# Where a split w_out lives, and from which block on the down products are made of parts

## The chip, the cores and the metric

The kernel runs on one core of a Trainium2 chip. The core has five engines that run side by side, each with its own queue of instructions in a fixed order: TensorE (PE in the profile, with its weight loads as PEld), VectorE (DVE), ScalarE (ACT), GpSimd (POOL) and SyncE (SP, which only starts transfers here). They wait for one another by semaphores. SBUF is the on-chip memory that all of them work on. PSUM is a small memory of eight banks into which TensorE writes its sums. The metric is the time of one execution on the device, in microseconds (us).

## The reference

Two stages follow one another. The first is an attention with polynomial sketches over q, k and v of shape (4 batches, 4 heads, 1088 positions, 32). The second is a feed-forward block with 128 inputs, 1536 hidden units and 128 outputs on all 4 x 1088 = 4352 tokens.

```
a, b  = S1 x, S2 x                      # 8 numbers each, for q and for k
phi   = outer(a, b)                     # 64 features
kv    = phi(k)^T v ;  z = sum phi(k)    # per batch and head
x     = (phi(q) kv) / (phi(q) z + 1e-6) # then (batch, head, pos, d) -> (token, 128)
out   = (silu(x w_gate) * (x w_val)) w_out
```

All inputs are float32 in the reference, with weights that may arrive as 64-bit floats. The result is float32.

## The kernel before, in words

The 4352 tokens are cut into blocks. Batch 0 makes three blocks of 384, 320 and 384 tokens. The other 3264 tokens make six blocks of 480 and one of 384. These seven are the list `line`, and `line[0]` is the first block of 480. The hidden units are cut into 12 chunks of 128, numbered j. For a pair (block i, chunk j) the gate and value products give 128 hidden units for the tokens of the block, and the down product adds their share to the outputs.

TensorE takes a float32 product in several passes (in the trace, two matmul instructions, `L1077`). It takes the type float32r in one pass, but with fewer bits. So the kernel writes some products as three products of parts. With CUT = 1 - 2^-13, BETA = 4096 and WHOLE = 1 + 1/4096, a number x becomes x1 = round(CUT x), x0 = x - x1 and xd = WHOLE x1 - x. A weight w becomes w1 = round(CUT w), wb = BETA (w - w1) and wd = w1 - wb. Then w x is WHOLE (w1 x1 + wb x0) - wd xd. The gate and value products of all blocks of `line` are made this way: `start_unit` (L983) makes the product of differences (L989), which ACT scales in PSUM (L992), and `finish_unit` (L994) adds the other two (L1001, L1002). ACT then makes the silu (L1004), and DVE the product of both sides, which is the hidden chunk (L1009).

The list `DOWN` (L888) says which down products are made of parts too. Before the change these are six chunks of `line[2]`, nine of each of `line[3]` to `line[5]`, and seven of the last block, 40 in all. For these, `cut_hidden` (L951) cuts the hidden chunk: ACT or DVE makes h1 (L968, L966), POOL h0 (L969) and DVE hd (L972). In `down` (L1054) three one-pass matmuls follow (L1069, L1071, L1072), into two PSUM banks. One of these holds the parts `wd hd`, along with the plain down products of the same block. As the parts enter the result with a minus sign, the plain ones have to be made of negated weights; these are kept in `scaled`. The other bank holds the rest, is copied out by ACT with the factor WHOLE (`copy_out`, L1095), and DVE joins both (`put_together`, L1105). A block without parts has one bank and goes straight to `store`, where DVE transposes it (L1131) and SP sends it off. All other down products are plain float32 (L1077).

`cut_down` (L903) cuts ten of the twelve chunks of w_out (`FINE`), in steps y = 20 to 29.

The order of all work is written out by hand. The loop at the end (`for y in range(END)`) has a step y for each pair of `line` and j, 84 in all: y = 0 to 11 belong to `line[0]`, 12 to 23 to `line[1]`, and so on. A step y puts on the queues: the start of unit y+1, the finish of unit y, and one down product. The down product lags five steps behind its hidden chunk (`len(todo) > min(5 + ...)`, with one step more before the first of `line[1]`, so that at y = 18 two are made). `add_to(before, y + 1, f)` and `add_to(behind, y + 1, f)` put work ahead of or behind the ACT and DVE work of a later step. A hidden chunk of step y that is cut gets h1 in step y + 1, h0 in y + 2 and hd in y + 3.

Between these, the attention of batches 1 to 3 is woven in by the generator `attentions` (L615): `parts_of` takes one piece of it in each step up to y = 19, then in every second step. At y = 4, 6, 20, 22 and 40 (`GROUPS`) come its matmuls. DVE makes the features (L377, in `key_features`), POOL adds them up (`feature_sums`, L547), and `query_step` makes the query side (L741 to L758). The token parts x1, x0, xd of the next block are cut in `cut_tokens` (L865, L868, L873).

The units' PSUM: `pair` (L122) hands out the least lately used of three pairs of banks. The pair of a unit comes free when DVE has made the product (L1009), and the unit three steps on writes the same pair. Bank `acc` and bank `g2` hold the down sums. Both `line[0]` and `line[1]` put theirs into `acc`; a block with parts uses both banks, and consecutive later blocks swap the two.

SBUF is full, so buffers are used again under a name (`tag`): a tile with the tag of an older one waits until that one has been read. Before the change, the parts of w_out live in the tag `room` (an early scratch), their low part in `late` (ten late hidden slots), `scaled` in `zs`. The parts of hidden chunks live in six sets of three slots in the tags `kld`, `qld`, `vld`, `kT`, `qT` (keys, queries, values and their transposes) and `late`.

Of the kernel before, what the change touches and what calls it, by code (L numbers as in the profile page):

```python
# [19 lines left out]
def kernel(  # L20
# [28 lines left out]
    nc = tc.nc  # L49
# [100 lines left out]
    wg = const.tile([P, NCH, P], FP32, name="wg")  # L150
    wv = const.tile([P, NCH, P], FP32, name="wv")
# [162 lines left out]
    slots = [(hbuf[:, k, :] if k < NH - NL else late[:, k - NH + NL, :]) for k in range(NH)]  # L314
# [300 lines left out]
    def attentions():  # L615
# [54 lines left out]
        for b in (2, 3):  # L670
# [232 lines left out]
    def cut_down():  # L903

        n = len(FINE)
        parts = const.tile([P, 3, n, D], F32R, tag="room", name="dparts", bufs=1)
        w1, wb, wd = (parts[:, k] for k in range(3))
        scaled = apool.tile([P, len(PLAIN), D], FP32, tag="zs", name="scaled")
        low = const.tile([P, n, D], FP32, tag="late", name="dlow", bufs=1)
        down_parts.update(w1=w1, wb=wb, wd=wd, scaled=scaled)  # L910
        rest = [(0, slice(0, 1)), (1, slice(1, 8, 2)), (5, slice(6, 7)), (6, slice(NCH - 1, NCH))]

        def high(c):
            nc.scalar.activation(w1[:, c], wo[:, FINE[0] :][:, c], AF.Copy, scale=CUT)

        def left(c):
            nc.gpsimd.tensor_tensor(
                out=low[:, c], in0=wo[:, FINE[0] :][:, c], in1=whole(w1[:, c]), op=ALU.subtract
            )

        def scale(c):
            nc.scalar.activation(wb[:, c], low[:, c], AF.Copy, scale=BETA)

        def differ(c):
            nc.gpsimd.tensor_tensor(
                out=wd[:, c], in0=whole(w1[:, c]), in1=whole(wb[:, c]), op=ALU.subtract
            )

        def other(k, c):
            m = len(range(NCH)[c])  # L930
            nc.scalar.activation(scaled[:, k : k + m, :], wo[:, c, :], AF.Copy, scale=-1.0)


        def exchange():
            for k, c in zip((1, 3, 4), (8, 9, 10)):
                PLAIN[k] = c
                nc.scalar.activation(scaled[:, k, :], wo[:, c, :], AF.Copy, scale=-1.0)

        add_to(behind, NCH * 5 + 8, exchange)

        a, b, c = slice(0, 3), slice(3, 6), slice(6, n)
        for step in (
            [(high, a)], [(left, a), (high, b)], [(left, b), (scale, a)], [(differ, a), (high, c)],
            [(left, c), (scale, b)], [(differ, b), (scale, c)], [(differ, c), (other, *rest[0])],
            [(other, *rest[1])], [(other, *rest[2]), (other, *rest[3])],
        ):
            for f, *args in step:
                f(*args)
            yield

    def cut_hidden(y, i, j):  # L951

        if not h_sets:
            x = []
# [450 lines left out]
    for y in range(END):  # L1405
# [16 lines left out]
        if y in range(20, 30):  # L1422
            next(down_steps, None)
# [43 lines left out]
```

## Time and profile before

| | before |
|---|---|
| time, median of 3 runs | 276.71 us (276.70 to 277.21) |
| span of the profiled execution (the page gives no other time for it) | 275.1 us |
| PE busy | 268.8 us, 98% |
| PEld busy | 200.5 us, 73% |
| DVE busy | 214.1 us, 78% |
| ACT busy | 193.6 us, 70% |
| POOL busy | 105.7 us, 38% |
| TensorE clock granted | 0.999 |
| plain down products on `hbuf` (L1077), 128x480 | 565 ns for each of two instructions, overlapping |
| products of parts (L1069, L1071, L1072), 128x480 | 379 to 382 ns each, overlapping |

Matmuls are pipelined: the duration of one is longer than the distance to the next. What a piece of work on the PE costs is therefore read from the starts in the chain of waits, and not from the mean durations. The chain of waits is followed back from the last instruction, and a line of it is a start, a length, an engine and a line of the kernel. A timeline lists an engine's instructions in order of time; the brackets at the end say how long the engine was idle before the instruction, and what ended that idle time.

### The profile page before, as it was taken

What the parts mean: (1) busy time and instruction counts of PE and PEld (TensorE: products, weight loads), DVE (VectorE), ACT (ScalarE), POOL (GpSimd) and SP (SyncE); (2) the same over time, 40 slices, a digit from 0 to 9 for tenths busy, and PEclk for the clock granted to TensorE, in tenths of its full rate; (3) what the DMA queues carried; (4) which work ended last, traced back from release to release, by engine and by line L of the source; (5) the groups of instructions that cost most, each with busy time, mean ns of one, the idle gap of its engine ahead of it and who ended that gap; (6) DMA issues with size and microseconds to landing.
All of it is one profiled execution on the core that took longest, in us unless ns stands there. A gap on an engine that the chain in (4) does not pass through costs nothing.

```text
span 275.1 us, 5788 instructions
## 1 busy us (share of the span) xinstructions
PE 268.8 (98%) x2191; PEld 200.5 (73%) x2191; DVE 214.1 (78%) x373; ACT 193.6 (70%) x349; POOL 105.7 (38%) x117
## 2 busy tenths in 40 slices
PE   7999999999999999999999999999999999999995
PEld 6645566666785786777577777867887888789994
DVE  3997988989788773887545766967987995998871
ACT  2468666462685686677479898769879888897880
POOL 3313422149350640260034353435535663553330
PEclk9999999999999999999999999999999999999999
DMA  6573196122231043000200020000100200010021
GB/s 191 172 216 87 49 270 200 60 104 62 62 88 23 4 111 99 2 0 0 38 12 4 1 38 0 0 2 11 26 2 0 36 1 0 13 25 1 2 36 29
DMA packets 26139, 14.30 MB, mean 52 GB/s; under 512 B 19840, under 2 KB 24192, under 8 KB 26112
## 3 DMA queue, kind: packets, MB, share of 16 engines
q1 hardware_dynamic: 25456, 13.84, 19.6%
q8 instruction: 17, 0.28, 0.4%
q10 hardware_dynamic: 656, 0.10, 0.2%
q14 instruction: 10, 0.08, 0.1%
HBM read 11.41 MB, written 2.23 MB: 50 GB/s over the span
## 4 chain that ended last, share of the span: by engine, by line
PE 93%; DVE 3%; DMA 2%; ACT 1%; issue 0%; SPq 0%
PE PS L1077 20%; PE PS L1001 14%; PE PS L989 14%; PE PS L1002 14%; PE PS L1025 12%; PE PS L1072 3%; PE PS L1071 3%; PE PS L1069 3%; PE PS L354 2%; PE PS L776 2%; PE PS L342 2%; DMA kld<-in_k_dram 2%; PE PS L388 2%; PE PS L1117 1%; PE PS L497 1%; PE PS L445 1%
## 5 line engine op out<-in xcount | busy, mean ns | idle before, releaser
L992 ACT ACTIVATE PS<-PS 128x960 f32<-128x960 f32 (+1 forms) x90 | 83.3, 926 | 29.8 <-PE PS L989 28.8
L1009 DVE SCALAR_TENSOR_TENSOR hbuf<-PS,sg 128x480 f32<-128x480 f32 (+1 forms) x87 | 55.2, 634 | 36.6 <-ACT sg L1004 36.1
L1004 ACT ACTIVATE sg<-PS 128x480 f32<-128x480 f32 (+1 forms) x90 | 49.6, 551 | 1.6 <-PE PS L1002 1.2
L1077 PE MATMUL PS<-hbuf,wo 128*128 128x480 f32 (+2 forms) x94 | 39.4, 516 | 0.0
L989 PE MATMUL PS<-xd,graw 128*128 128x480 f32 (+1 forms) x69 | 37.5, 543 | 0.0
L989 PE MATMUL PS<-xd,wd 128*128 128x480 f32 (+1 forms) x90 | 33.6, 373 | 0.0
L1002 PE MATMUL PS<-x,wb 128*128 128x480 f32 (+1 forms) x90 | 33.5, 372 | 0.0
L1001 PE MATMUL PS<-x,w 128*128 128x480 f32 (+1 forms) x90 | 33.4, 371 | 0.0
L1002 PE MATMUL PS<-x,graw 128*128 128x480 f32 (+1 forms) x69 | 25.5, 370 | 0.0
L989 PEld LDWEIGHTS PS<-xd,wd 128*128 128x128 f32 x90 | 17.0, 189 | 9.9 <-issue 5.3
L1025 PE MATMUL PS<-xT,wg 128*128 128x384 f32 (+1 forms) x60 | 23.5, 473 | 0.1
L1025 PE MATMUL PS<-xT,wv 128*128 128x384 f32 (+1 forms) x60 | 23.2, 467 | 0.3 <-DVE wv L286 0.3
L868 POOL TENSOR_TENSOR x<-xT,x 128x480 fp32r<-128x480 f32 (+1 forms) x6 | 7.2, 1195 | 37.8 <-ACT x L865 37.8
L1077 PEld LDWEIGHTS PS<-hbuf,wo 128*128 128x128 f32 x94 | 17.7, 189 | 5.4 <-issue 0.4
L1029 ACT ACTIVATE sg<-PS 128x384 f32<-128x384 f32 (+1 forms) x24 | 11.2, 468 | 13.2 <-PE PS L1025 12.4
L969 POOL TENSOR_TENSOR hlate<-hbuf,hlate 128x480 fp32r<-128x480 f32 (+1 forms) x12 | 14.6, 1218 | 11.0 <-ACT hlate L968 9.7
L989 PEld LDWEIGHTS PS<-xd,graw 128*128 128x128 f32 x69 | 13.0, 188 | 7.6 <-ACT PS L992 4.1
L1001 PEld LDWEIGHTS PS<-x,w 128*128 128x128 f32 x90 | 16.9, 187 | 2.2
L1002 PEld LDWEIGHTS PS<-x,wb 128*128 128x128 f32 x90 | 16.9, 188 | 2.1
L1001 PE MATMUL PS<-x,graw 128*128 128x480 f32 (+1 forms) x48 | 18.1, 376 | 0.0
L1077 PE MATMUL PS<-hbuf,scaled 128*128 128x480 f32 (+1 forms) x40 | 17.1, 518 | 0.0
L1025 PEld LDWEIGHTS PS<-xT,wv 128*128 128x128 f32 x60 | 11.2, 190 | 7.4 <-DVE hbuf L1040 0.8
(205 smaller groups left out, 572.0 us busy)
## 6 DMA issues: line engine op xcount, KB each, us to landing
kld<-in_k_dram SPq DMA_DIRECT2D x4, 544.0 KB, 4.4
vld<-in_v_dram SPq DMA_DIRECT2D x12, 144.0 KB, 4.3
qld<-in_q_dram SPq DMA_DIRECT2D x3, 544.0 KB, 4.8
raw<-in_moe_w_out_dram SPq DMA_DIRECT2D x4, 384.0 KB, 4.4
raw<-in_moe_w_gate_dram SPq DMA_DIRECT2D x3, 384.0 KB, 3.3
raw<-in_moe_w_val_dram SPq DMA_DIRECT2D x3, 384.0 KB, 3.5
out_dram<-o SPq DMA_DIRECT2D x16, 60.0 KB, 2.0
vld<-in_v_dram SPq DMA_DIRECT2D x4, 112.0 KB, 4.1
```

What stands on the lines that cost most here:

```text
L969: add_to(before, y + 2, lambda: nc.gpsimd.tensor_tensor(out=h0, in0=h, in1=whole(h1), op=ALU.subtract))
L989: nc.tensor.matmul(ps[:, k], w_parts[id(w), j // 3][2][:, j % 3, :], xd, start=True, stop=True)
L992: nc.scalar.activation(ps, ps, AF.Copy, scale=-1.0 / WHOLE)
L1001: nc.tensor.matmul(ps[:, k], w1, x1, start=False, stop=False, skip_group_check=True)
L1002: nc.tensor.matmul(ps[:, k], wb, x0, start=False, stop=True, skip_group_check=True)
L1004: nc.scalar.activation(sg, ps[:, 0], AF.Silu, scale=WHOLE)
L1009: nc.vector.scalar_tensor_tensor(out=hj[:, 0:n], in0=ps[:, 1], scalar=WHOLE, in1=sg, op0=ALU.mult, op1=ALU.mult)
L1025: nc.tensor.matmul(o[:, 0:n], w[:, j, :], xT[:, t0 : t0 + n], start=True, stop=True)
L1029: nc.scalar.activation(sg[:, 0:n], g[:, 0:n], AF.Silu)
L1069: nc.tensor.matmul(acc[i][:, 0:n], wd, hd, **sides)
L1071: nc.tensor.matmul(p, w1, h1, start=(j == mine[0]), stop=False)
L1077: nc.tensor.matmul(acc[i][:, 0:n], w, hidden[i, j][:, 0:n], **sides)
```

## The change

Three things are done together. The parts of w_out move into `wg` and `wv`, the buffers of the gate and value weights, which have been read out by then (their own parts lie elsewhere), and `zs`; their low part gets a buffer of its own, `low`, taken from `room`. They are cut in five pieces from y = 5, 6, 13, 14 and 23 on. The difference of weights is made with the other sign, wb - w1, so that plain products need no negated weights: `scaled` and its copies go, and the join becomes a plain addition. The parts of hidden chunks get seven sets (five before `line[2]`) in `room`, `late`, `kld` + `kT`, `kT` + `qld`, `vld` + `qT` and `feats`; `feats` is the part of `late` that had held the features of batch 3. With this, `DOWN` gets three chunks of `line[0]`, five of `line[1]`, and nine of `line[2]` where there were six: 51 in all. Both `line[0]` and `line[1]` now use the two banks and a join. In `line[0]` and `line[2]` DVE makes h1 of chunk 8, in `line[1]` of 6, 8 and 10; ACT makes the others.

Lines after the change are 15 or 16 lower from `cut_hidden` on: L974 and L977 for L989 and L992, L989 for the silu L1004, L994 for the unit product L1009, L950, L948, L951 and L954 for the cuts of hidden chunks, L1054, L1056, L1057 and L1061 for the down products, L1079, L1089 and L1113 for copy, join and transpose. L910, L912, L914 and L916 are the cuts of w_out.

```diff
-    wg = const.tile([P, NCH, P], FP32, name="wg")
-    wv = const.tile([P, NCH, P], FP32, name="wv")
+    wg = const.tile([P, NCH, P], FP32, tag="wg", name="wg", bufs=1)
+    wv = const.tile([P, NCH, P], FP32, tag="wv", name="wv", bufs=1)
...
-    NL = 10
+    NL, NF = 10, 6
-    late = const.tile([P, NL, BW], FP32, tag="late", name="late", bufs=1)
+    late = const.tile([P, NL - NF, BW], FP32, tag="late", name="late", bufs=1)
+    feats = const.tile([P, NF, BW], FP32, tag="feats", name="feats", bufs=1)
...
-                phk = late[:, NL - 6 :, :].rearrange("p s (n h i j) -> p (s n) h i j", h=1, i=R, j=R)
+                phk = feats[:].rearrange("p s (n h i j) -> p (s n) h i j", h=1, i=R, j=R)
...
-    FINE, PLAIN = range(1, NCH - 1), [0, 1, 3, 5, 7, 6, NCH - 1]
-    DOWN = [(line[2], j) for j in (2, 4, 6, 8, 9, 10)]
-    DOWN += [(i, j) for i in line[3:6] for j in (1, 2, 4, 5, 6, 7, 8, 9, 10)]
+    DOWN = [(line[0], j) for j in (6, 8, 10)] + [(line[1], j) for j in range(6, 11)]
+    DOWN += [(i, j) for i in line[2:6] for j in (1, 2, 4, 5, 6, 7, 8, 9, 10)]
...
+    def cut_down(c0, c1, home, low):
+        n = c1 - c0
+        w1, wb, wd = (home[:, n * k : n * k + n, :] for k in range(3))
+        for k in range(n):
+            down_parts[c0 + k] = [x[:, k, :] for x in (w1, wb, wd)]
+        src = wo[:, c0:c1, :]
+        nc.scalar.activation(w1, src, AF.Copy, scale=CUT)
+        yield
+        nc.gpsimd.tensor_tensor(out=low, in0=src, in1=whole(w1), op=ALU.subtract)
+        yield
+        nc.scalar.activation(wb, low, AF.Copy, scale=BETA)
+        yield
+        nc.gpsimd.tensor_tensor(out=wd, in0=whole(wb), in1=whole(w1), op=ALU.subtract)
+
+    def more_room():
+        def ground(tag, n):
+            t = const.tile([P, n, WB], F32R, tag=tag, name="h" + tag, bufs=1)
+            return [t[:, k, :] for k in range(n)]
+        x = ground("room", 6)
+        yield x[:3]
+        yield x[3:]
+        yield ground("late", 3)
+        x = ground("kld", 2) + ground("kT", 2)
+        yield x[:3]
+        x = x[3:] + ground("qld", 2)
+        yield x
+        x = ground("vld", 2) + ground("qT", 2)
+        yield x[:3]
+        yield ground("feats", 4)[:3]
...
-        if not h_sets:
...
+        if len(h_sets) < (5 if i < line[2] else OWN):
+            h_sets.insert(0, next(h_rooms))
...
-        if j in (2, 5, 8, 10) and i != line[2]:
+        if j in ((2, 5, 8, 10) if i > line[2] else (6, 8, 10) if i == line[1] else (8,)):
...
-            w1, wb, wd = [down_parts[x][:, FINE.index(j), :] for x in ("w1", "wb", "wd")]
+            w1, wb, wd = down_parts[j]
...
-            w = down_parts["scaled"][:, PLAIN.index(j), :] if mine else wo[:, j, :]
-            nc.tensor.matmul(acc[i][:, 0:n], w, hidden[i, j][:, 0:n], **sides)
+            nc.tensor.matmul(acc[i][:, 0:n], wo[:, j, :], hidden[i, j][:, 0:n], **sides)
...
-        join = lambda: nc.vector.scalar_tensor_tensor(
-            out=x, in0=d, scalar=-1.0, in1=x, op0=ALU.mult, op1=ALU.add
-        )
+        join = lambda: nc.vector.tensor_tensor(out=x, in0=d, in1=x, op=ALU.add)
...
-    down_steps = cut_down()
+    for y0, c0, c1, where in (
+        (5, 5, 8, ("wg", 0)), (6, 8, 11, ("wv", 0)), (13, 4, 5, ("wg", 9)), (14, 1, 2, ("wv", 9)),
+        (23, 2, 4, ("zs", 0)),
+    ):
+        for k in range(4):
+            down_steps.setdefault(y0 + k, []).append((k, c0, c1, *where))
...
-        if y in range(20, 30):
-            next(down_steps, None)
+        for k, c0, c1, tag, t0 in down_steps.get(y, ()):
+            if k == 0:
+                n = c1 - c0
+                parts_at = settle(tag, NCH if tag != "zs" else 6)[:, t0 : t0 + 3 * n, :]
+                low_at = settle("low", 6)[:, 3 * (c0 >= 8) :, :][:, 0:n, :]
+                cutting[c0] = cut_down(c0, c1, parts_at, low_at)
+            next(cutting[c0], None)
```

More of the change, by code (lines that the diff above doesn't have):

```diff
@@ L310 @@
     NH = 27
-    NL = 10
+    NL, NF = 10, 6
     hbuf = const.tile([P, NH - NL, BW], FP32, name="hbuf")
-    late = const.tile([P, NL, BW], FP32, tag="late", name="late", bufs=1)
-    slots = [(hbuf[:, k, :] if k < NH - NL else late[:, k - NH + NL, :]) for k in range(NH)]
+    late = const.tile([P, NL - NF, BW], FP32, tag="late", name="late", bufs=1)
+    feats = const.tile([P, NF, BW], FP32, tag="feats", name="feats", bufs=1)
+    slots = [x[:, k, :] for x, n in ((hbuf, NH - NL), (late, NL - NF), (feats, NF)) for k in range(n)]
     slot_of = {}
@@ L901, in now @@
             f()
[L903 to L918, printed above, removed]
-            )
[L921 to L949, printed above, removed]
@@ L951, in cut_hidden @@
-    def cut_hidden(y, i, j):
-        if not h_sets:
-            x = []
-            for tag in ("kld", "qld", "vld", "kT", "qT"):
-                t = const.tile([P, 2, WB], F32R, tag=tag, name="h" + tag, bufs=1)
-                x += [t[:, k, :] for k in range(2)]
-            t = const.tile([P, 8, WB], F32R, tag="late", name="hlate", bufs=1)
-            x += [t[:, k, :] for k in range(8)]
-            h_sets.extend(x[k : k + 3] for k in range(0, 18, 3))
+    def cut_down(c0, c1, home, low):
[11 more added lines that the diff above has]
+        nc.gpsimd.tensor_tensor(out=wd, in0=whole(wb), in1=whole(w1), op=ALU.subtract)
@@ L961, in cut_hidden @@
+    h_rooms = more_room()
+    OWN = 7
+    def cut_hidden(y, i, j):
+        if len(h_sets) < (5 if i < line[2] else OWN):
+            h_sets.insert(0, next(h_rooms))
         n = SPLIT if i == LAST else blocks[i][1]
@@ L974, in cut_hidden @@
         ))
-    room = const.tile([P, 10, BW], FP32, tag="room", name="room", bufs=1)
+    rooms = [
+        const.tile([P, n, BW], FP32, tag=tag, name=tag, bufs=1) for tag, n in (("room", 8), ("low", 2))
+    ]
+    room = [x[:, k, :] for x, n in zip(rooms, (8, 2)) for k in range(n)]
     sums_of = {}
@@ L1027, in unit @@
             )
-        sg = room[:, len(lates) + caught[0], :] if late else fpool.tile([P, WB], FP32, tag="sg", name="sg", bufs=5)
+        sg = room[len(lates) + caught[0]] if late else fpool.tile([P, WB], FP32, tag="sg", name="sg", bufs=5)
         nc.scalar.activation(sg[:, 0:n], g[:, 0:n], AF.Silu)
@@ L1104, in put_together @@
         acc[i] = x
-        join = lambda: nc.vector.scalar_tensor_tensor(
-            out=x, in0=d, scalar=-1.0, in1=x, op0=ALU.mult, op1=ALU.add
-        )
+        join = lambda: nc.vector.tensor_tensor(out=x, in0=d, in1=x, op=ALU.add)
         if i == LAST:
@@ L1294, in free @@
     def free(c):
-        return [room[:, c, :].rearrange("p (c f) -> p c f", f=P)]
+        return [room[c].rearrange("p (c f) -> p c f", f=P)]
     w = ("wg", "wv")
@@ L1403, with settle @@
             token_steps.setdefault(at, []).append(gen)
-    down_steps = cut_down()
+    home = {}
+    def settle(tag, n=NCH):
+        if tag not in home:
+            pool = apool if tag == "zs" else const
+            home[tag] = pool.tile([P, n, D], FP32 if tag == "low" else F32R, tag=tag, name="d" + tag, bufs=1)
+        return home[tag]
+    down_steps = {}
+    for y0, c0, c1, where in (
[4 more added lines that the diff above has]
+            down_steps.setdefault(y0 + k, []).append((k, c0, c1, *where))
+    cutting = {}
     for y in range(END):
```

## The prediction

> **What bounds the kernel now.** I read the page first, for busy shares and clock, then the chain of waits in order of time, then the timelines of PE, DVE and POOL around the blocks that change.
>
> ```profile
> PE 268.8 (98%) x2191; PEld 200.5 (73%) x2191; DVE 214.1 (78%) x373; ACT 193.6 (70%) x349; POOL 105.7 (38%) x117
> PEclk9999999999999999999999999999999999999999
> PE 93%; DVE 3%; DMA 2%; ACT 1%; issue 0%; SPq 0%
> ```
>
> TensorE is busy for 98% of the span at full clock, and 93% of the chain is its own work. So time is won or lost in two ways only: PE work that goes away, and a PE that has to stand still. The chain of waits shows what a step of the fused loop costs (each line is the start of a step's two difference matmuls, or its down product):
>
> ```profile
> 110.02 0.44 PE PS L989 x2
> 111.33 0.80 PE PS L1077 x2
> 112.14 0.44 PE PS L989 x2
> ...
> 204.76 0.43 PE PS L989 x2
> 206.72 0.43 PE PS L989 x2
> 208.66 0.43 PE PS L989 x2
> ```
>
> A step with a plain fp32 down product takes 112.14-110.02 = 2.12 us. A step whose down product is made of parts (L1069 to L1072) takes 1.94 to 1.96 us. Elsewhere plain steps are 2.10 to 2.12 (120.58, 122.69, 124.79). In both places the PE starts nothing late. A product of parts is therefore worth about 0.15 us, in bounds 0.14 to 0.18.
>
> What stands beside the PE where the first new parts come is VectorE, steps 8 to 13 of the loop (step y=9 starts at 112.14):
>
> ```profile
> 111.95 0.66 DVE L1009 SCALAR_TENSOR_TENSOR hbuf<-PS,sg 128x480 f32<-128x480 f32 x1 [0.84 <-ACT sg L1004]
> 112.53 0.95 DVE L377 TENSOR_TENSOR late<-kab 128x768 f32<-128x768 f32 x1
> 113.39 0.65 DVE L873 SCALAR_TENSOR_TENSOR xd<-x,xT 128x480 fp32r<-128x480 f32 x1
> 114.07 0.66 DVE L1009 SCALAR_TENSOR_TENSOR hbuf<-PS,sg 128x480 f32<-128x480 f32 x1
> 114.65 1.28 DVE L377 TENSOR_TENSOR late<-kab 128x512 f32<-128x512 f32 x2
> 116.19 0.66 DVE L1009 SCALAR_TENSOR_TENSOR hbuf<-PS,sg 128x480 f32<-128x480 f32 x1 [0.26 <-ACT sg L1004]
> ...
> 118.88 1.57 DVE L741 TENSOR_TENSOR dot<-qab 128x288 f32<-128x288 f32 x1
> ```
>
> Here DVE makes the next batch's features between the products of the hidden units, with hardly a gap: the busy times by stretch give it 9.71 of 10.77 us between 111.95 and 122.72.
>
> How late may it be? The product of y=9 ends at 114.65 and frees the PSUM pair that the start of unit y=12 writes at 116.38: 1.7 us of slack. Beyond that the PE stands.
>
> The last view is the price of DVE next to POOL:
>
> ```profile
> 162.40 0.62 DVE L972 SCALAR_TENSOR_TENSOR hqld<-hkld,hbuf 128x480 fp32r<-128x480 f32 x1
> 195.60 1.48 DVE L972 SCALAR_TENSOR_TENSOR hlate<-hlate,hbuf 128x480 fp32r<-128x480 f32 x1
> ...
> 195.34 1.22 POOL L969 TENSOR_TENSOR hlate<-hbuf,hlate 128x480 fp32r<-128x480 f32 x1 [0.74 <-ACT hlate L968]
> ```
>
> The same difference takes 0.62 us beside an idle POOL and 1.48 us when it starts inside a POOL operation. It ends at 197.08, half a microsecond after POOL's end at 196.56: it waited POOL out and then ran. Transposes don't: L1131 at 189.42 took 0.67 beside a POOL operation of 189.37 to 190.61.
>
> **The change, part by part.**
>
> *Parts instead of plain products.* Before, 6 + 27 + 7 = 40 down products are of parts; after, 3 + 5 + 36 + 7 = 51. Eleven more times 0.15 is 1.65 us of PE work gone (1.54 to 1.98 by the bounds). PE has no other new work, and every later step moves forward by what it saved.
>
> *Cutting w_out.* Ten slices are cut before and after, four operations each way, now in five pieces instead of three, at y=5 to 9, 13 to 17 and 23 to 26 instead of 20 to 29. ACT pays 10 operations of 0.31 to 0.53 for 6 of 0.51 to 0.64; POOL 10 of about 0.4 (one slice, scaled from 1.02 for three) to 1.02 for 6 of 1.01 to 1.28. None is on the PE's path. The first set's last operation comes at y=8, by my estimate from the ACT and POOL rows at about 112.5, and the first product that reads it at y=11, about 117.7: 5 us of cover. ACT is 8.89 of 12.68 busy there. Taken: 0. If the cover went, one step of 2.1 us would be waited.
>
> *Negated copies.* The seven slices of `scaled` and the later exchange (7 ACT operations of 0.31 to 0.63, at 155 to 161 and 243) go; the sign moves into `wd`. ACT had slack there (0.1 to 0.5 us idle in most steps), so the PE gains nothing: 0. It makes room for two more ACT cuts in the third block.
>
> *Cutting eleven more hidden units.* Each costs a copy with CUT (ACT 0.61, or DVE 0.40), a POOL subtraction (1.22) and a DVE difference (0.62 to 1.48). ACT gets 6, DVE 5 of the copies. Two more blocks also get a copy of sums on ACT (0.57) and a join on DVE (0.65). On ACT a step is 0.87 + 0.45 + 0.48 = 1.8 us start to start with a cut in it, under 1.95: 0. On POOL, 4.5 us busy of 20 between 100 and 120 and 1.7 of 20 after that: 0 for POOL itself. On DVE it is the doubtful part:
> - y=8 to 13 gets three differences and one copy: 3 x 0.64 + 0.40 = 2.3 us clean. Idle time of 1.06 and the slack of 1.7 hold 2.8 us: then nothing is lost.
> - But POOL gets three subtractions and two differences of w_out into the same stretch, 5 x 1.0 to 1.2 us, beside the sums of features that it already does. A DVE operation caught costs some 0.75 more (1.40 against 0.65; 1.05 more for a feature product: 2.00 at 172.59 against 0.95). All six catchable ones caught (three differences at 0.75, one copy at 0.88, two feature products at 1.05) make 2.3 + 5.2 = 7.5, and the PE would stand 4.7 us. None caught: 0. I take one and a half caught, since a transpose or a PSUM-fed product often takes the place beside POOL: 2.3 + 1.1 - 2.8 = 0.6 us.
> - y=14 to 19 has 1.5 us idle up to y=16, and gets one join (0.65) and four small POOL operations. The join is a new wait: the first down product of the second block writes the bank that it reads, at 131.61. Before, the transpose had freed that bank at 130.1. Now the join stands behind a transpose (130.0 to 130.9 by the rows) and ends near 130.9 against a PE that is 0.45 us earlier, 131.2. Behind it on DVE's queue are the unit product, the second transpose of features, and so the numerators at 135.33 (before, ready at 133.92). Bounds 0 to 0.65, and it is the same lateness as above, not a second one. Taken: within the 0.6.
> - Third block (y=24 to 36), nine differences beside three feature products and three transposes. The stretch 169.94 to 180.8 already runs so: the caught 2.00 us product makes the next unit late by under 1 us, and the following transposes win it back. Bounds 0 to 1.0 us; taken 0, nearest to that row.
>
> *Rooms.* `late` is cut into two buffers, `room` into two; parts live where keys, queries, values and features have been read out. The only new waits on transfers are for v and q of the last batch, loaded a dozen steps earlier. SP's queue keeps its order. 0.
>
> Sum: -1.65 + 0.6 = -1.05. The profiled execution has a span of 275.1; the page shows no other time for it, and the median of the runs is 276.71, so 1.6 us lie around the span. 276.71 - 1.05 = 275.66; I say **275.6**.
>
> The Trainium skill, "SBUF — State Buffer", section "Who interferes with whom", says that a DVE instruction with two SBUF inputs and a GpSimd instruction that reads SBUF lock each other out whole. It speaks against this change, and the two L972 rows agree with it (0.62 and 1.48). By the rule alone, if POOL were never idle in those steps, all six would be caught and the time would be 276.71 - 1.65 + 4.7 = 279.8.
>
> **Rivals.**
> - *Nothing stands in the way.* The differences fall into POOL's gaps: 276.71 - 1.65 = 275.06. For it: DVE runs at 22.20 of 25 us between 193 and 218 with nine parts in twelve steps and no PE wait. Against: no features were made there.
> - *The gain is eaten.* Two to three and a half are caught between y=8 and 19: the PE stands 1.0 to 2.1 us, result 276.1 to 277.2. The break-even is where 2.3 + 0.75 n - 2.8 = 1.65: n = 2.9.
> - *DVE becomes the bound of the first two blocks, and the kernel is slower.* One mechanism: POOL's subtractions and DVE's feature products catch each other at y=9 to 13, so the PSUM pairs come free late. From four caught on it is 2.5 us of standing, 277.6. Against: a PE that stands gives DVE time to catch up, and transposes are not held.
> - *The parts of w_out are late* and the product at y=11 waits: one step, 276.71 - 1.65 + 2.1 = 277.2. The 5 us of cover speak against it; under 2%, counted with the eaten gain.
>
> **How the numbers follow.** The forecast (0.3 to 1.0 us given back, 275.35 to 276.05) has 0.34, no wait 0.33, gain eaten 0.15, slower 0.18. A measurement of this kernel can tell about 0.2%, 0.55 us, from no change. Faster is the first two, 0.67; within 0.2% 0.14; slower 0.19, with the upper edge of the eaten case. The range goes from 274.9 (eleven times 0.165 and no wait) to 277.4, which takes in the eaten case and leaves out the bulk of the slower one.
>
> **What would show it.** Right: 51 products of parts; steps of 1.96 us with L1054 to L1057 in the first block's tail (y=11, 13, 15) and in the second's (y=23 to 27); no `scaled`; PE busy 267 us or so; DVE differences of 1.2 to 1.5 us beside POOL at 112 to 125 and unit products (L994) there up to 2 us behind their ACT partner; a pause of the PE of some tenths before a start of a unit at 116 to 126. Wrong: PE pauses above 1.6 us in sum before 136; a pause before the second block's first down product, or before the numerators at 135, as large; a step with parts that takes no less than a plain one; ACT as the last waited for.

## The result

The changed kernel takes **280.24 us** (median of 4 runs, 279.98 to 280.85) against 276.71 us before (276.70 to 277.21): a ratio of 1.0129, with a 95% interval of 1.0114 to 1.0144. It is slower by 3.5 us. The prediction said 275.6, in a range of 274.9 to 277.4, and was wrong. The profiled execution took 280.44 us, with a span of 278.4, which is 3.3 more than the 275.1 of before.

The page of the changed kernel, in the same parts as those shown of before: busy times, granted clock, shares of the chain, and the group of difference matmuls, which before had no idle time ahead of it:

```profile
PE 269.1 (97%) x2202; PEld 201.8 (72%) x2202; DVE 228.6 (82%) x391; ACT 196.2 (70%) x354; POOL 122.6 (44%) x132
PEclk9999999999999999999999999999999999999999
PE 86%; DVE 9%; DMA 2%; issue 1%; ACT 1%; SPq 0%
L974 PE MATMUL PS<-xd,wd 128*128 128x480 f32 (+1 forms) x90 | 34.4, 382 | 3.2 <-DVE hbuf L994 3.2
```

The clock is full, so it is not that. DVE is 14.5 us busier and POOL 16.9. DVE's share of the chain that ended last went from 3% to 9%. The last line says where the PE stands: at the start of units, 3.2 us in all, until DVE has made a hidden chunk (L994) and thereby freed a PSUM pair. Here is that part of the chain, in order of time, in the first and the third block of 480 tokens:

```profile
114.20 0.45 PE PS L974 x2
114.68 0.96 ACT PS L977
115.69 0.64 DVE hbuf L994
116.33 1.46 DVE feats L378 x2
118.14 0.65 DVE hbuf L994
118.79 1.12 DVE feats L378
119.91 1.58 DVE hroom L954
121.49 0.58 DVE hbuf L994
122.11 0.48 PE PS L974
...
174.15 1.31 DVE hroom L954
175.95 1.42 DVE phq L378
177.58 1.31 issue
178.89 0.65 DVE hbuf L994
179.59 0.48 PE PS L974
```

Before, this chain ran along the PE through the whole stretch. Now it leaves the PE in these places and runs along DVE: unit product, feature products, a late difference, unit product, and only then the PE.

**Where the time went.** Let S(y) be the start of the difference matmul `xd,wd` in step y, from the timelines of the PE. The lateness of S(y) in the new kernel against S(y) before, stretch by stretch, gives the table below. A product of parts should pull the later steps forward by 0.15 us, so the PE's standing time is the net plus 0.15 for each new product in that stretch. Both executions have S(0) within 0.08 us of each other.

| stretch | net lateness gained | new products of parts | standing time |
|---|---|---|---|
| S(0) to S(20), first block | +2.23 | 3 | 2.7 |
| S(20) to S(30), second block | -0.03 | 5 | 0.7 |
| S(30) to S(41), third block | +1.27 | 3 | 1.7 |
| S(41) to S(82) | -0.10 | 0 | 0 |
| sum | +3.38 | 11 x 0.15 = 1.65 | 5.1 |

So the gain is there, and is eaten three times over. Single steps show it best. Where nothing is in the way, the distance from one step to the next is 0.13 to 0.16 us shorter than before at S(24), S(25), S(26) and S(31). It is longer by 0.35 at S(12), 1.17 at S(13), 0.66 at S(15), 0.35 at S(27), and 0.12 and 1.21 at S(36) and S(37).

**What DVE does there.** The timeline of DVE in the first block after the change:

```profile
112.61 1.70 DVE L378 TENSOR_TENSOR feats<-kab 128x768 f32<-128x768 f32 x1
114.23 0.65 DVE L874 SCALAR_TENSOR_TENSOR xd<-x,xT 128x480 fp32r<-128x480 f32 x1
114.80 0.65 DVE L954 SCALAR_TENSOR_TENSOR hroom<-hroom,hbuf 128x480 fp32r<-128x480 f32 x1
115.37 0.40 DVE L948 TENSOR_SCALAR hroom<-hbuf 128x480 fp32r<-128x480 f32 x1
115.69 0.64 DVE L994 SCALAR_TENSOR_TENSOR hbuf<-PS,sg 128x480 f32<-128x480 f32 x1
116.26 1.96 DVE L378 TENSOR_TENSOR feats<-kab 128x512 f32<-128x512 f32 x2
118.14 0.65 DVE L994 SCALAR_TENSOR_TENSOR hbuf<-PS,sg 128x480 f32<-128x480 f32 x1
118.71 1.20 DVE L378 TENSOR_TENSOR feats<-kab 128x512 f32<-128x512 f32 x1
119.83 1.66 DVE L954 SCALAR_TENSOR_TENSOR hroom<-hroom,hbuf 128x480 fp32r<-128x480 f32 x1
121.42 0.64 DVE L994 SCALAR_TENSOR_TENSOR hbuf<-PS,sg 128x480 f32<-128x480 f32 x1
...
125.14 1.18 DVE L954 SCALAR_TENSOR_TENSOR hlate<-hlate,hbuf 128x480 fp32r<-128x480 f32 x1
```

and POOL's in the same time (the bracket is idle time and what ended it):

```profile
112.49 1.01 POOL L916 TENSOR_TENSOR dwv<-dwv 128x384 fp32r<-128x384 f32 x1
115.85 1.22 POOL L951 TENSOR_TENSOR hroom<-hbuf,hroom 128x480 fp32r<-128x480 f32 x1 [2.35 <-DVE hroom L948]
117.79 1.58 POOL L548 TENSOR_TENSOR zs<-feats 128x512 f32<-128x512 f32 x1 [0.72 <-PE PS L987]
119.51 1.47 POOL L951 TENSOR_TENSOR hlate<-hbuf,hlate 128x480 fp32r<-128x480 f32 x1
```

One more line of the kernel before is needed, the last feature product of this group:

```profile
116.77 0.87 DVE L377 TENSOR_TENSOR late<-kab 128x512 f32<-128x512 f32 x1
```

Five operations of DVE start inside an operation of POOL and last longer than the same operation did before (for the differences, which are new, longer than the 0.65 of the one at 114.80): the feature product at 112.61 by 0.75 (1.70 against 0.95 before) beside the cut of w_out; the two at 116.26 by 0.68 (1.96 against 1.28) beside h0 of chunk 8; the one at 118.71 by 0.33 (1.20 against 0.87, which ran beside the sums before, too) beside the sums of features; the difference at 119.83 by 1.01 beside h0 of chunk 10, and the one at 125.14 by 0.53 beside the end of the sums. That is 3.3 us. Against it, two operations that the sums of features held up before are freer now (L742 0.95 instead of 1.57, L747 0.23 instead of 0.48), and L749 is held by 0.2 more: 2.6 us net. With 2.3 us of clean new work, against the 2.8 us of room that the prediction worked out, 2.1 us are left over; the PE stood 2.7. The other 0.6 us would be room that couldn't be used, such as idle time ahead of the first delay; no run shows that. The operation at 115.85 shows why this is no accident: what released POOL is DVE's own copy of the hidden chunk, so POOL starts on h0 just as DVE turns to its feature products. (Of the three h0 of this block, this one alone waits for a copy on DVE; the other two follow a copy on ACT.) POOL loses time as well: the h0 at 119.51, which starts inside a feature product, takes 1.47 us against 1.22.

The timeline of the PE shows the last part of each delay as a wait for L994, and no other wait between 111 and 128 us:

```profile
118.84 0.48 PE L974 MATMUL PS<-xd,wd 128*128 128x480 f32 x1 [0.23 <-DVE hbuf L994]
122.11 0.48 PE L974 MATMUL PS<-xd,wd 128*128 128x480 f32 x1 [0.89 <-DVE hbuf L994]
126.95 0.49 PE L974 MATMUL PS<-xd,wd 128*128 128x480 f32 x1 [0.49 <-DVE hbuf L994]
...
179.59 0.48 PE L974 MATMUL PS<-xd,wd 128*128 128x480 f32 x1 [1.20 <-DVE hbuf L994]
```

In the third block three operations in a row are caught, with only a unit product between the first two:

```profile
174.07 1.39 DVE L954 SCALAR_TENSOR_TENSOR hroom<-hroom,hbuf 128x480 fp32r<-128x480 f32 x1
175.95 1.42 DVE L378 TENSOR_TENSOR phq<-qab 128x768 f32<-128x768 f32 x1
177.29 1.68 DVE L954 SCALAR_TENSOR_TENSOR hlate<-hlate,hbuf 128x480 fp32r<-128x480 f32 x1
```

POOL makes an h0 from 173.73 to 174.95, from 174.92 to 176.55 and from 176.80 to 178.45. Against 0.65, 0.95 and 0.65 these three operations lose 2.2 us.

The brackets of the PE are shorter than the time lost. The matmul before the one at 122.11 ran from 120.47 to 121.23, and its successor would have started 0.59 us after it, as it did before, inside its run; and after the pause the next matmul starts 0.32 us later, where otherwise it is 0.22. So 0.89 + 0.16 + 0.10 = 1.15 of the 1.17 us by which step 13 is longer.

### The profile page after: what moved, and what is told of

Same layout as the page of the kernel before. It is cut to its first block, busy times and chain, and to the rows that moved or that the text cites. A ratio compares the mean times of both kernels' runs of the same rounds, so it can differ in the third digit from the quotient of the medians.

```text
span 278.4 us, 5854 instructions
## 1 busy us (share of the span) xinstructions
PE 269.1 (97%) x2202; PEld 201.8 (72%) x2202; DVE 228.6 (82%) x391; ACT 196.2 (70%) x354; POOL 122.6 (44%) x132
## 3 DMA queue, kind: packets, MB, share of 16 engines
HBM read 11.41 MB, written 2.23 MB: 49 GB/s over the span
## 4 chain that ended last, share of the span: by engine, by line
PE 86%; DVE 9%; DMA 2%; issue 1%; ACT 1%; SPq 0%
PE PS L1061 16%; PE PS L974 13%; PE PS L986 13%; PE PS L987 12%; PE PS L1010 12%; PE PS L1056 3%; PE PS L1054 3%; PE PS L1057 3%; DVE hbuf L994 2%; PE PS L355 2%; PE PS L777 2%; PE PS L343 2%; PE PS L389 2%; DMA kld<-in_k_dram 2%; DVE hroom L954 2%
## 5 line engine op out<-in xcount | busy, mean ns | idle before, releaser
L977 ACT ACTIVATE PS<-PS 128x960 f32<-128x960 f32 (+1 forms) x90 | 83.3, 926 | 28.7 <-PE PS L974 27.7
L994 DVE SCALAR_TENSOR_TENSOR hbuf<-PS,sg 128x480 f32<-128x480 f32 (+1 forms) x87 | 54.8, 631 | 25.6 <-ACT sg L989 23.1
L989 ACT ACTIVATE sg<-PS 128x480 f32<-128x480 f32 (+1 forms) x90 | 49.7, 552 | 1.6 <-PE PS L987 1.2
L1061 PE MATMUL PS<-hbuf,wo 128*128 128x480 f32 (+3 forms) x112 | 45.9, 507 | 0.0
L974 PE MATMUL PS<-xd,wd 128*128 128x480 f32 (+1 forms) x90 | 34.4, 382 | 3.2 <-DVE hbuf L994 3.2
L974 PE MATMUL PS<-xd,graw 128*128 128x480 f32 (+1 forms) x69 | 35.2, 510 | 0.0
L974 PEld LDWEIGHTS PS<-xd,wd 128*128 128x128 f32 x90 | 16.9, 188 | 13.7 <-DVE hbuf L994 7.6
L951 POOL TENSOR_TENSOR hroom<-hbuf,hroom 128x480 fp32r<-128x480 f32 (+1 forms) x16 | 20.0, 1253 | 13.0 <-ACT hroom L950 7.1
L1061 PEld LDWEIGHTS PS<-hbuf,wo 128*128 128x128 f32 x112 | 20.9, 189 | 5.7 <-issue 0.4
L987 PEld LDWEIGHTS PS<-x,wb 128*128 128x128 f32 x90 | 16.9, 188 | 2.2
L986 PEld LDWEIGHTS PS<-x,w 128*128 128x128 f32 x90 | 16.9, 188 | 2.2
L974 PEld LDWEIGHTS PS<-xd,graw 128*128 128x128 f32 x69 | 13.0, 188 | 6.6 <-ACT PS L977 2.8
L954 DVE SCALAR_TENSOR_TENSOR hroom<-hroom,hbuf 128x480 fp32r<-128x480 f32 (+1 forms) x16 | 16.7, 1047 | 0.0
L1010 PEld LDWEIGHTS PS<-xT,wg 128*128 128x128 f32 x60 | 10.9, 190 | 7.7 <-issue 1.1
```

Of the source, the lines that this page charges most:

```text
L951: add_to(before, y + 2, lambda: nc.gpsimd.tensor_tensor(out=h0, in0=h, in1=whole(h1), op=ALU.subtract))
L954: add_to(before, y + 3, lambda: nc.vector.scalar_tensor_tensor(out=hd, in0=whole(h1), scalar=WHOLE, in1=h, op0=ALU.mult, op1=ALU.subtract))
L974: nc.tensor.matmul(ps[:, k], w_parts[id(w), j // 3][2][:, j % 3, :], xd, start=True, stop=True)
L977: nc.scalar.activation(ps, ps, AF.Copy, scale=-1.0 / WHOLE)
L986: nc.tensor.matmul(ps[:, k], w1, x1, start=False, stop=False, skip_group_check=True)
L987: nc.tensor.matmul(ps[:, k], wb, x0, start=False, stop=True, skip_group_check=True)
```

## The experiments

The theory after the result: DVE and POOL hold each other up where both read SBUF, and the PE stands only by what DVE's own added work and what POOL holds up exceed the room together. The rival: DVE's own added work alone is too much. All runs but two make the whole computation; what these two leave out is said with them. "Standing time" is worked out as above, for the profiled execution of each kernel, and stands in one table at the end of this section.

### One block without parts, one with six

The first undoes the three products of parts of the first block alone, the second brings the third block back to its six:

```diff
-    DOWN = [(line[0], j) for j in (6, 8, 10)] + [(line[1], j) for j in range(6, 11)]
+    DOWN = [(line[1], j) for j in range(6, 11)]
```

> The three products of parts of the first 480-token block are plain again; the early cuts of w_out stay. Both theories of a late VectorE (its own added work, or POOL locking it out) expect the standing of the PE before y=20 to go: the step y=20 starts at most 0.5 us later than before (+2.15 with the change), and the time is near 280.2 - 2.1 = 278.1. If the early cuts of w_out alone made the block late, only about 0.5 us is won: 279.7.

```diff
-    DOWN += [(i, j) for i in line[2:6] for j in (1, 2, 4, 5, 6, 7, 8, 9, 10)]
+    DOWN += [(line[2], j) for j in (2, 4, 6, 8, 9, 10)]
+    DOWN += [(i, j) for i in line[3:6] for j in (1, 2, 4, 5, 6, 7, 8, 9, 10)]
```

> The third 480-token block has its six products of parts as before, not nine; all else as changed. If the three added ones make VectorE late there, the stand at y=36 to 37 goes and the time is near 280.2 - 1.3 = 278.9. If the stand comes from what runs over from the second block, or from the last cut of w_out, it stays and the time is near 280.2 + 0.0 to 0.5.

Measured: 278.37 us (278.30 to 278.84), ratio 1.0070 (1.0047 to 1.0093) without the first block's, and 279.68 (279.06 and 280.29), 1.0107 (1.0049 to 1.0166) with six in the third. The standing time of just the block that was changed back goes to zero, and the others keep theirs (2.6 to 2.7, 0.6 to 0.8 and 1.7). So the losses of the first and the third block are separate, and each comes from that block's own new parts. Without the first block's parts the cut of w_out still holds up the feature product (1.70 us at 112.40), the last feature product takes 1.21 against 0.87, and S(20) is as early as before: these delays alone fit into the room.

### What holds DVE up: POOL's h0 left out, DVE's hd left out

In the first and third block, POOL's h0 isn't computed and h1 stands in its place; DVE's instructions stay as they are. In the third block this takes away all nine h0, also the six that were there before the change:

```diff
-        add_to(before, y + 2, lambda: nc.gpsimd.tensor_tensor(
-            out=h0, in0=h, in1=whole(h1), op=ALU.subtract
-        ))
+        if i in (line[0], line[2]):
+            h_parts[i, j] = [h1, h1, hd]
+        else:
+            add_to(before, y + 2, lambda: nc.gpsimd.tensor_tensor(
+                out=h0, in0=h, in1=whole(h1), op=ALU.subtract
+            ))
```

> Left out: POOL's subtraction h0 in the first and third 480-token blocks (h1 stands in its place in the product, so the output is not the reference's there). VectorE has every instruction that it has with the change; POOL has 12 fewer. Lock theory: the differences there run in 0.6 to 0.7 us, the PE stands under 0.8 us instead of 2.6 before y=20 and under 0.5 instead of 1.8 after, time near 280.2 - 1.8 - 1.4 = 277.0. Theory that VectorE's own added work is too much: nothing moves, 280.2.

Measured: 277.29 us (276.85 to 277.56, 8 runs), ratio 1.0016 (1.0005 to 1.0027). With the same number of DVE instructions the third block has no standing time, and all three of its gains appear (0.15 to 0.16 at S(31), S(35) and S(37)). There the rival falls. In the first block 1.6 us are left, twice the 0.8 that was expected at most, and the timeline of DVE shows what is behind them: the delays by h0 are gone, and those by the cut of w_out and by the sums of features are not.

```profile
112.83 1.70 DVE L378 TENSOR_TENSOR feats<-kab 128x768 f32<-128x768 f32 x1
...
116.48 1.28 DVE L378 TENSOR_TENSOR feats<-kab 128x512 f32<-128x512 f32 x2
...
118.24 1.22 DVE L378 TENSOR_TENSOR feats<-kab 128x512 f32<-128x512 f32 x1
119.39 1.73 DVE L957 SCALAR_TENSOR_TENSOR hroom<-hroom,hbuf 128x480 fp32r<-128x480 f32 x1
```

The opposite run leaves POOL everything, and takes DVE's differences away:

```diff
-        add_to(before, y + 3, lambda: nc.vector.scalar_tensor_tensor(
-            out=hd, in0=whole(h1), scalar=WHOLE, in1=h, op0=ALU.mult, op1=ALU.subtract
-        ))
+        if i in (line[0], line[2]):
+            h_parts[i, j] = [h1, h0, h0]
+        else:
+            add_to(before, y + 3, lambda: nc.vector.scalar_tensor_tensor(
+                out=hd, in0=whole(h1), scalar=WHOLE, in1=h, op0=ALU.mult, op1=ALU.subtract
+            ))
```

> The changed kernel with DVE's difference hd left out in the first and third block (h0 stands in its place, so those blocks' outputs miss the middle parts of the product); POOL does all that it did, and the products of parts stay. Theory (DVE's own added work plus what POOL holds up, together against 2.8 us of room): without the three differences the first block has left one copy (0.40) and POOL's hits on the feature products and copies, some 1.8 to 2.2 us in all, under the room: the stand in the first block is 0 to 0.6 us instead of 2.6, the third block's goes as well, and the time is 276.6 to 277.8. Rival (POOL's hits on the attention's own feature products are enough without the differences): the first block's stand stays above 1.5 us and the time above 278.5.

Measured: 275.71 us (275.68 to 276.36), ratio 0.9967 (0.9951 to 0.9983), below the range that was expected, since in both blocks all the gains show. The feature products are held up just as much (1.70, 1.96 and 1.21 us in its timeline), yet the PE stands 0.15 us in the first block and not at all in the third. In the third block, then, neither POOL's h0 alone nor DVE's differences alone make the PE wait, only both together. In the first, POOL's operations without the differences cost 0.15 us; the differences with no POOL operation beside them were not run there.

### Moving POOL's work within the first block

The first two cuts of w_out start at y = 3 and 4 instead of 5 and 6:

```diff
-        (5, 5, 8, ("wg", 0)), (6, 8, 11, ("wv", 0)), (13, 4, 5, ("wg", 9)), (14, 1, 2, ("wv", 9)),
+        (3, 5, 8, ("wg", 0)), (4, 8, 11, ("wv", 0)), (13, 4, 5, ("wg", 9)), (14, 1, 2, ("wv", 9)),
```

> The first two cuts of w_out start at y=3 and 4 instead of 5 and 6, so that POOL is done with them before VectorE makes the features of batch 3 at y=8. Lock theory: the feature product of y=8 takes 0.95 us instead of 1.70, the lateness at y=11 to 13 falls by 0.75, and so does the time: 279.5. Theory of VectorE's own work: no change, 280.2. If ScalarE is too full at y=3 and 4, up to 0.5 us is lost there.

Measured: 279.45 us (279.34 and 279.55), ratio 1.0099 (1.0070 to 1.0129). The feature product is free of POOL again:

```profile
112.42 0.95 DVE L378 TENSOR_TENSOR feats<-kab 128x768 f32<-128x768 f32 x1
```

It saves 0.75 there, and the standing time of the first block falls from 2.7 to 1.7.

Next, with that cut, the sums of features are handed to POOL three pieces of the attention later:

```diff
-    def beside(gen, steps):
+    def beside(gen, steps, k=0):
...
-        for x in gen:
-            if steps:
+        for n, x in enumerate(gen):
+            if steps and n >= k:
...
-            yield from beside(query_step(b, qab), sums)
+            yield from beside(query_step(b, qab), sums, 3)
```

> All 51 products of parts, but POOL is kept away from VectorE's busy steps of the first block: the first two cuts of w_out start at y=3 and 4, and the sums of the features of batch 3 are handed out three pieces of attention later (y=14 to 17 instead of 11 to 14). VectorE's instructions and their order are those of the change. Lock theory: the difference of (first block, 8) takes 0.65 us instead of 1.66 and the feature product beside it 0.7 instead of 1.2, the stand of 2.6 us before y=20 falls to under 0.5, the step y=20 starts within 0.3 us of before, and the time is near 280.2 - 2.2 = 278.0. Theory of VectorE's own work: 279.5, as with the early cuts alone, or 280.2.

Measured: 279.50 us (279.35 and 279.64), ratio 1.0098 (1.0078 to 1.0118), 1.5 above what was expected. In the first block most of the standing time goes: the last feature product takes 0.68, the difference after it 0.65, and 0.4 us are left. The sums now catch two feature products of the queries instead (1.89 and 1.72 us against 0.95), later, where DVE had more idle time. But the profiled execution was 1.31 us late at S(0) already, before anything that differs. Its 36 key products, the PE's first work on k, took 2.19 us instead of 1.49: two of them started every 0.107 us all through, where in the changed kernel it is mostly every 0.058. The trace's record of the full TensorE clock begins 9.90 us after the start of the span, and between 3.8 and 6.4 us in all other profiles; in the last kernel of this section, where it begins at 6.43, the distance falls from 0.107 to 0.059 at that moment. So the PE worked at about half its pace in these products; what kept the clock back isn't shown. By this estimate the profiled execution would have taken 279.35 - 1.31 = 278.04 us without the late start, which is what was expected.

### The second block alone, and two ways to spread the parts

```diff
-    DOWN = [(line[0], j) for j in (6, 8, 10)] + [(line[1], j) for j in range(6, 11)]
-    DOWN += [(i, j) for i in line[2:6] for j in (1, 2, 4, 5, 6, 7, 8, 9, 10)]
+    DOWN = [(line[1], j) for j in range(6, 11)]
+    DOWN += [(line[2], j) for j in (2, 4, 6, 8, 9, 10)]
+    DOWN += [(i, j) for i in line[3:6] for j in (1, 2, 4, 5, 6, 7, 8, 9, 10)]
```

> Only the second block's five products of parts are added (none in the first, six in the third as before); rooms, cuts and signs as changed. The PE gains 5 x 0.15 = 0.75 us and stands 0.4 to 0.5 at y=26 (as with the change): 276.71 - 0.3 = 276.4, within 0.2% of before. If moving the parts of w_out, the rooms and the sign cost something by themselves, it is slower than before by that much.

Measured: 276.69 us (276.28 to 277.03, 10 runs) against 276.97 before on the same chip, ratio 0.9990 (0.9979 to 1.0002). The new rooms, the cuts of w_out, the sign and the second block's join cost nothing that can be seen in the first and third block, which stand 0.0. The five products of the second block gain 0.75, and the PE stands 0.65 there. In the changed kernel it waits there for a unit product too (0.34 us before 157.79), which stands behind two caught differences: 1.40 us at 153.10, beside an h0, and 1.20 at 155.98, beside a cut of w_out. No run leaves out POOL's work in this block alone.

Then three sets of changes together. The first keeps the edits of the last section, gives the third block eight parts without chunk 7, with all its copies on ACT, and cuts the last piece of w_out at y = 25:

```diff
+    DOWN += [(line[2], j) for j in (1, 2, 4, 5, 6, 8, 9, 10)]
...
+        (25, 2, 4, ("zs", 0)),
```

> As the run with late sums, and in the third block eight products of parts (1, 2, 4, 5, 6, 8, 9, 10; chunk 7 plain), the copy of its chunk 8 on ScalarE, and the last cut of w_out at y=25 to 28 instead of 23 to 26. Ten products more than before, worth 1.5 us on the PE. Lock theory: all stands fall to under 0.5 us in sum, 275.2 to 276.2, faster than before. If VectorE's work itself is the bound, 277 to 278.

Measured: 277.18 us (276.99 to 277.56, 10 runs), ratio 1.0009 (0.9994 to 1.0025). That misses the 275.2 to 276.2 of the theory and lies in the range of its rival; the PE stands 2.0 us in sum, 0.75 of them in the second block, which nothing here had eased. The old place in the third block is clear, and 0.9 us are lost in a new one, at S(33): with h0 of the next chunks the same meeting happens again, on DVE and on POOL:

```profile
164.28 1.96 DVE L378 TENSOR_TENSOR phq<-qab 128x768 f32<-128x768 f32 x1
166.16 1.66 DVE L955 SCALAR_TENSOR_TENSOR hkT<-hkld,hbuf 128x480 fp32r<-128x480 f32 x1
```

```profile
164.21 1.22 POOL L952 TENSOR_TENSOR hqld<-hbuf,hkT 128x480 fp32r<-128x480 f32 x1 [0.62 <-ACT hkT L951]
166.05 1.27 POOL L952 TENSOR_TENSOR hroom<-hbuf,hroom 128x480 fp32r<-128x480 f32 x1 [0.62 <-ACT hroom L951]
```

The second puts the second block's parts on chunks 4, 5, 6, 7 and 9, gives the third seven, and makes all cuts of w_out but the last from y = 3 to 5 on, with the sums late:

```diff
+    DOWN = [(line[0], j) for j in (6, 8, 10)] + [(line[1], j) for j in (4, 5, 6, 7, 9)]
+    DOWN += [(line[2], j) for j in (1, 2, 4, 6, 8, 9, 10)]
...
+        (3, 5, 8, ("wg", 0)), (4, 8, 11, ("wv", 0)), (4, 4, 5, ("wg", 9)), (5, 1, 2, ("wv", 9)),
```

> Products of parts placed where VectorE has room: first block 6, 8, 10 as changed, second block 4, 5, 6, 7, 9 (their differences fall beside the attention's matmuls at y=20 and 22), third block 1, 2, 4, 6, 8, 9, 10; the first four cuts of w_out from y=3, 4, 4, 5, the sums of batch 3 handed out three pieces later. Nine products more than before, 1.35 us of PE work less. Lock theory: only the first block is still caught (sums beside the difference of chunk 10), 0.5 us of standing; 276.71 - 0.85 = 275.9. If chunks 4 and 5 of the second block make the numerators at y=20 late, 276.4.

Measured: 278.01 us (277.79 to 279.56), ratio 1.0063 (1.0040 to 1.0086). The second and third block stand no longer. The first does, for 2.4 us: the sums now fell on `qab` (1.19 us) and on a difference (1.73), and h0 of the second block's chunk 4 on a feature product of the queries (2.00 us), so that the transposed features and a unit product behind them came late for the numerators at y = 20 (the PE waits 0.34 and 0.66 us for them). The theory had 0.5 us and 275.9.

The third is the same without parts in the first block, and with the sums where they were:

```diff
+    DOWN = [(line[1], j) for j in (4, 5, 6, 7, 9)]
```

> The same without the first block's three products and with the sums where they were: six products more than before, 0.9 us of PE work less. Lock theory: no stand over 0.2 us is left that was not there before; 276.71 - 0.9 = 275.8, faster than both kernels. If the stand at y=26 does not come from the differences of chunks 8 and 10 but from the second block's parts as such, 276.2.

Measured: 276.33 us (275.94 to 277.55, 11 runs) against 276.60, ratio 0.9991 (0.9980 to 1.0003). It stands at one place, 0.56 us at S(20), where the numerators wait for a unit product behind the same late feature product. Again this place was not foreseen; 275.8 was expected.

### Four and five parts in the second block, seven in the third

Chunk 4 of the second block goes, and with it the h0 beside the queries' feature product; the fifth part is then put at chunk 10:

```diff
+    DOWN = [(line[1], j) for j in (5, 6, 7, 9)]
```

> No parts in the first block (line[0]); second block 5, 6, 7, 9; third block 1, 2, 4, 6, 8, 9, 10; the first cuts of w_out at y=3, 4, 4, 5. Against g2 only the second block's unit 4 goes: its POOL copy h0 lay beside the feature product phq at 131.4 (1.97 us) and PE stood 0.55 us at y=20. Theory (DVE and POOL lock each other out, and PE stands only where DVE is then over 1.7 us late): no stand anywhere; 45 products of parts, 5 more than before, 5 x 0.15 = 0.75 us less: 275.9 to 276.1, step y=20 no later than before. Rival (the second block has no room for parts whatever their place, since DVE has its own work there): a stand of 0.3 to 0.6 us remains between y=19 and 28, and the time is 276.3 to 276.6.

```diff
+    DOWN = [(line[1], j) for j in (5, 6, 7, 9, 10)]
```

> As the run with 5, 6, 7, 9 in the second block, with 10 as well: 46 products of parts. Theory: the product of parts 10 hands a DVE difference and a POOL copy into the steps at y=25 to 27, where the changed kernel stood 0.3 us at S(27) with five in a row (6 to 10). If those five in a row were the cause, a gap at 8 is enough and this gives 0.15 less than the other, 275.8; if the one at 10 alone is (its difference meets the next batch's first work), the stand of 0.3 us at y=27 comes back and the time is 0.1 to 0.2 above the other.

Measured: 276.30 us (276.04 to 277.90, 12 runs), ratio 0.9988 (0.9971 to 1.0005) with four, and **275.81 us** (275.68 to 276.19, 5 runs), ratio 0.9966 (0.9954 to 0.9978) with five. The queries' feature product is free now; the timelines with chunk 4 and without it:

```profile
131.37 1.97 DVE L378 TENSOR_TENSOR phq<-qab 128x768 f32<-128x768 f32 x1
```

```profile
131.42 0.95 DVE L378 TENSOR_TENSOR phq<-qab 128x768 f32<-128x768 f32 x1
```

In both kernels the PE stands nowhere by more than 0.1 us from S(0) to S(41). With four, the time is above the 275.9 to 276.1 of the theory and at the lower end of its rival's range, but the stand of 0.3 to 0.6 us that the rival needs isn't there; with five it is what was expected. Five with a gap at chunk 8 don't bring back the 0.35 us at S(27) that five in a row cost, so chunk 10 wasn't the cause there. By the steps, each of the six new products saves 0.15 (at S(28) the kernel with chunk 10 gains 0.15 on the other). The last kernel is faster than the one before by 0.9 us (276.72 on the same chip), and than the changed one by 4.4 (measured on another chip). Its page answers to the first lines of both:

```profile
PE 268.1 (98%) x2197; PEld 201.7 (74%) x2197; DVE 220.2 (80%) x383; ACT 194.3 (71%) x350; POOL 114.1 (42%) x127
PE 93%; DVE 3%; ACT 2%; issue 0%
```

All runs by their standing times, in us, worked out from the profiled executions (0.15 for each new product of parts added to the net lateness):

| kernel | median | new parts by block | first, S(0)-S(20) | second, S(20)-S(30) | third, S(30)-S(41) |
|---|---|---|---|---|---|
| the changed kernel | 280.24 | 3, 5, 3 | 2.7 | 0.7 | 1.7 |
| no parts in the first block | 278.37 | 0, 5, 3 | 0.0 | 0.6 | 1.7 |
| third block with six | 279.68 | 3, 5, 0 | 2.6 | 0.8 | 0.0 |
| h0 left out, first and third | 277.29 | 3, 5, 3 | 1.6 | 0.7 | 0.0 |
| hd left out, first and third | 275.71 | 3, 5, 3 | 0.15 | 0.7 | 0.0 |
| early cut | 279.45 | 3, 5, 3 | 1.7 | 0.75 | 1.75 |
| and late sums | 279.50 | 3, 5, 3 | 0.4 | 0.7 | 1.75 |
| and third block spread | 277.18 | 3, 5, 2 | 0.4 | 0.75 | 0.9 |
| second block alone | 276.69 | 0, 5, 0 | 0.0 | 0.65 | 0.0 |
| all blocks eased | 278.01 | 3, 5, 1 | 2.4 | 0.1 | 0.0 |
| the same without the first | 276.33 | 0, 5, 1 | 0.6 | 0.0 | 0.0 |
| four and seven | 276.30 | 0, 4, 1 | 0.0 | 0.1 | 0.0 |
| five and seven | 275.81 | 0, 5, 1 | 0.0 | 0.0 | -0.1 |

## Why the prediction was wrong, by its steps

- **"11 x 0.15 = 1.65":** right. Each new product shortens its step by 0.13 to 0.16 us wherever nothing stands in the way; in the run without hd this holds in the first block as well.
- **"None is on the PE's path", the cutting of w_out:** right by itself (the second block alone: 0.0 us in the first block). But one of its POOL operations met a feature product, 0.75 us, and taking that away saved 1.0 us of standing. It belongs to the next step.
- **"I take one and a half caught", the 0.6 us at y = 8 to 13: here it failed.** The clean work of 2.3 us and the room of 2.8 held to within 0.6. The price of a catch held (0.66 us in the mean, 0.75 assumed); the count didn't. Five operations were caught up to y = 15, for 3.3 us (2.6 net of what became freer), and not one and a half for 1.1. The reason given for the low number, that a transpose or a PSUM-fed product often takes the place beside POOL, didn't hold: the h0 of chunk 8 is released by the copy that DVE makes just ahead of its feature products, and the sums of features are released by these products themselves (in the kernel before, and in the run without h0, the profile names them). The term was 0.6 us and measured 2.7. The sum with the 2.6 that was caught gives 2.1; why it was 0.6 more stays open.
- **"Taken: within the 0.6", the join and numerators at y = 14 to 19:** right. From S(16) to S(20) the lateness stays at 2.07 to 2.15 us, so the join moved nothing.
- **"Bounds 0 to 1.0 us; taken 0", the third block: failed too.** It measured 1.7, above the upper bound. The nearest row that I went by, one caught feature product of 2.00 us that the PE didn't feel, came from a block with six parts; with nine a difference of 1.39, a feature product of 1.42 and a difference of 1.68 follow each other, 2.2 us too long together, and no transpose lies between them and the unit product at 178.89. Without h0 these delays and the standing time are gone.
- **The second block, y = 20 to 28, had no term of its own** and costs 0.7 us, 0.5 of them in one step at S(27): it is 0.35 longer than before and was to be 0.15 shorter.
- **Rooms and negated copies, 0:** right (the second block alone contains both).
- **The rivals.** The third, DVE as the bound of the first two blocks, is what happened, and its 2.5 us for the first block is near the 2.7 measured, in part by luck: with the delays as measured its working gives 2.1. It had a chance of 0.18 and no term for the later blocks: 276.71 - 1.65 + 2.7 + 0.7 + 1.7 = 280.2. What spoke against it, that a standing PE lets DVE catch up, is true within a step (S(14) and S(16) lose only 0.1 of their gain), but the next meeting with POOL comes before the room is there again.

"SBUF — State Buffer" of the Trainium skill, section "Who interferes with whom", says that a DVE instruction with two SBUF inputs and a GpSimd instruction that reads SBUF exclude each other for the whole instruction, and that the order of issue decides who waits. The rows agree (0.65 beside 1.66, and 0.95 beside 1.97, for the same shape), and so does the run without h0, in which the third block's delays vanish with POOL's operations. The sum by that rule with all six caught, 279.8 us, came nearest to the result, by luck, since the distribution is another: it had 4.7 us in the first block, where 2.7 were measured, and nothing in the others.

## What to carry to other kernels

Where two engines hold each other up, count the meetings from the order of release, not from the share of time in which the second is busy: work that an engine releases for an idle one starts beside whatever stands next in its own queue. Work out the room of each stage (idle time plus what may be late before a buffer is missed) and add both sides to it, new work and delays. In these runs the gain of 0.15 us per product was kept where the PE did not stand. Picking such places by trial (five products in the second block, seven in the third, none new in the first) gave 0.9 us, where taking all cost 3.5.

## What the runs showed that I had not expected

- The place of a meeting is decided by tenths of a microsecond. Handing the sums to POOL three pieces later freed two operations and caught two others, which the PE hardly felt (0.4 us). With other parts beside it, the same edit caught two other operations, which with the delayed numerators left 2.4 us of standing. In both runs the move that took one meeting away made another.
- Executions differ before the changed part, though the computations up to there are the same. In twelve of the thirteen kernels that were compared with the one before, S(0) lay between 0.4 us earlier and 0.14 later, in step with the start of DVE's first transposes of k, which wait for a transfer (5.29 to 5.85 us). In the one with late sums it lay 1.31 later, and there the PE's clock rose late. Differences of some tenths between two kernels therefore come from the steps, and not from the total alone.
- The same delay of 0.75 us on a feature product costs nothing where there is room (no parts in the first block) and 1.0 us where the room is used up already (early cut against the changed kernel): a delay has no price of its own.
